# The first rows' normalization in a spectral and token-mixing kernel: Newton steps moved from GpSimd to VectorE, a longer first memset, and buffers exchanged in the later stages

## The chip, the core and the metric

The kernel runs on one core of one Trainium2 chip. The metric is device time in microseconds (us), from launch to the end of the program; the median of a few runs is compared. The core has TensorE (PE in the profile, with PEld for its weight loads), VectorE (DVE), ScalarE (ACT), GpSimd (POOL), and SyncE (SP), which issues most of the loads. ACT and POOL have DMA queues of their own beside SP's. Each engine runs its instructions in the order in which they were issued to it, and waits on semaphores for what the others produce.

## What is computed

```
xn = layernorm(x)                               x: 2048 x 640, fp32
a  = xn @ dft_hid_re.T ;  b = xn @ dft_hid_im.T             (640 x 640)
yA = dft_seq_re @ a - dft_seq_im @ b                        (2048 x 2048)
h  = layernorm(xn)
u  = gelu(h.T @ w1 + b1)                                    (640 x 1728)
yB = (u @ w2 + b2).T                                        (2048 x 640)
out = x + yA + yB
```

Two branches share the input: a Fourier mixing along both axes, and a mixer MLP along the token axis. Both begin with the layer norm of x.

## The kernel before

**Precision and splitting.** Every product is made from fp32 operands split in two: a high part rounded to the matmul's input type (`high`, an ACT copy, L151) and the low part, the rest (`low`, a VectorE subtraction, L154). Each product is three passes of matmuls: high with high, high with low, low with high (`three`, L162, L163, L165; `products` in the first columns, L511). Large products are done in the Strassen-Winograd manner, with 7 products of blocks in place of 8; the sums of blocks are VectorE's (`sub`, L157) and are spread between the steps.

**Steps.** The work is a list of steps. A step takes one tile of matrix rows ("piece", 128 x 512 or so), lets ACT make its top (high part) two steps ahead, VectorE its bottom (low part), and TensorE the matmuls. `turn_of` issues a turn in this order: loads, reads of finished banks, sums, the top of the step two ahead, extras, timed jobs, the bottom, what stands behind it, and then the step's matmuls. `JOBS_AT` and `LONG_AT` say in which turns a job from the waiting list is taken; loads, jobs and reads are hung on steps by number (`loads`, `timed`, `extras`, `behind_lo`).

**Stages.** First come the products of x with the sequence matrices (`first_columns` for the first block of 512 columns and the rows that arrive first, then `columns` for seven more blocks), stored to a scratch tensor y; then the hidden-axis products (`hidden`), then the up-projection (`up`, two stages) and the down-projection (`down`, two stages). Large buffers are eight "slabs" of on-chip memory, which take turns: rows of x with high and low parts (`fixed`), then the moving operands (`moving_of`), matrices (`load_matrices`) or extra pieces (`more`). A tile given a slab's tag waits for the last reader of the tile before it. Smaller pair buffers (`place`: v, ca, cb, x0, x1, x2) hold results that are summed up. Partial results of the up-projection go to a scratch tensor in HBM (`part_up`) from POOL's queue, and are summed there by the DMA.

**The start** is written out by hand in `START`, one word for one helper: `x` loads a row block of x (128 tokens x 640), `b` a piece of the matrices, `M` the two halves of the moments (L223), `A` their aggregate (L226), `R` the inverse root on ACT (L232), `O` the offset from it, `D` and `H` the high parts of a row's blocks, `N` the normalized row itself (ACT, L278), `L` the low parts (VectorE), `T` and `B` top and bottom of a step's piece, `P` the matmuls of a step, with a list of passes if not all three. The root from ACT's table is refined by a Newton step: three small operations and the offset. For rows 2, 3, 6 and 7 it is on VectorE (`F`: L238 to L240, L254). For rows 0, 1, 4 and 5 it is on POOL, in `factors_beside` (word `V`, L248 to L250 and L243), and the first offset too (`O`, L243). Row 0 is loaded in two halves (L536).

The first matrix piece, b0, is loaded from ACT's queue, behind a one-column memset of its tile (L498), so that the load waits for VectorE. Before the first real matmul, `WARM` matmuls on a zero tile run (L148): ten of 512 columns and four of 128.

The ten steps of `first_columns` are listed in `FIRST`. In the first step of both outputs the third pass stands last (`P0-0-1 P1-0-1 P0-2 P1-2`). Steps 0 to 5 are issued in `START`; from step 6 on the turns are made by `turn_of`. At the head of turn 6 ACT copies the first output's five banks (`read`, L519). Step 6 begins the second output's blocks 3 and 4 in banks 0 and 1, which the first output has used.

Of the kernel before, what the change touches and what calls it, by code (L numbers as in the profile page):

```python
# [8 lines left out]
F32 = mybir.dt.float32  # L9
# [15 lines left out]
G = 4  # L25
# [3 lines left out]
EPS = 1e-5  # L29
AHEAD = 2  # L30
LOADS = 4
WARM = 14

BLOCK = 10
APART = 2
# [12 lines left out]

START = """
    x0 b0 W0 b1 x1 b2 x4 b3 x5 b4 x2 x3 b5 x6 x7 b6 b7  # L50
    M0 A0 R0 T0 D0 O0 V0 H0 B0 T1 B1 M1 A1 N0 R1 T2 L0 O1 V1 H1 B2 P0-0-1 P1-0-1 P0-2 P1-2
    M4 A4 R4 N1 O4 V4 L1 T3 H4 B3 M5 A5 N4 R5 O5 V5 T4 P2
    L4 B4 P3 H5 T5 M2 A2 N5 M3 A3 R2-3 B5 F2-3 L5 q4 P4
    H2 T6 N2 M6 A6 B6 L2 q5 P5 T7 M7 B7 A7
"""


# [20 lines left out]
def fnet_plus_mixer(  # L78
# [38 lines left out]
    b2_sb = keep.tile([P, NS], F32, name="b2_sb")  # L117
    one = keep.tile([P, 1], F32, name="one")
    eps = keep.tile([P, 1], F32, name="eps")
    idea = keep.tile([P, 1], F32, name="idea")  # L120

    mv = keep.tile([P, NS, 2], F32, name="mv")
    norm = keep.tile([P, 2, NS], F32, name="norm")
# [16 lines left out]
    nc.vector.memset(idle, 0.0)  # L140
    nc.vector.memset(one, 1.0)
    nc.gpsimd.memset(eps, EPS)
    nc.gpsimd.tensor_scalar(idea, eps, EPS, eps, op0=ALU.add, op1=ALU.mult)
    psum = [acc.tile([P, CH], F32, name=f"psum{i}") for i in range(8)]
    for i in range(WARM):
        n = 4 if i < WARM - 4 else 1
        to = psum[7][:, : n * P].rearrange("p (n c) -> p n c", n=n)
        nc.tensor.matmul(to, idle, idle.unsqueeze(1).to_broadcast([P, n, P]), start=True, stop=True)  # L148

# [67 lines left out]

    stats = {}

    def statistics(k, row):  # L220
        stats[k] = small.tile([P, 2, 6], F32, name="st")
        for i in range(2):
            nc.vector.bn_stats(stats[k][:, i, :], row[:, i * H2 : (i + 1) * H2])  # L223

    def aggregate(k):
# [16 lines left out]
    def offset_beside(to, k):  # L242
        nc.gpsimd.tensor_scalar(to[:, 1, k : k + 1], mv[:, k, 0:1], to[:, 0, k : k + 1], -1.0, op0=ALU.mult, op1=ALU.mult)  # L243

    def factors_beside(k):

        r, q = small.tile([P, 1], F32, name="beside"), near[:, 0, k : k + 1]
        nc.gpsimd.tensor_scalar(r, mv[:, k, 1:2], EPS, q, op0=ALU.add, op1=ALU.mult)  # L248
        nc.gpsimd.tensor_scalar(r, r, q, -0.5, op0=ALU.mult, op1=ALU.mult)  # L249
        nc.gpsimd.tensor_scalar(norm[:, 0, k : k + 1], r, 1.5, q, op0=ALU.add, op1=ALU.mult)  # L250
        offset_beside(norm, k)

    def offset(to, ks):
        nc.vector.scalar_tensor_tensor(to[:, 1, ks], mv[:, ks, 0], -1.0, to[:, 0, ks], op0=ALU.mult, op1=ALU.mult)  # L254
# [103 lines left out]
    for q in range(4):  # L358
        place_fixed(0, q)

    def first_rows(k, which):
# [17 lines left out]
        for to, t in whole:  # L379
# [36 lines left out]
    def later_row(k):  # L416
        return later_pair(k % 4)[:, (k - 8) // 4, :]
# [69 lines left out]
    def first_columns():  # L487
# [6 lines left out]
        def load(i):  # L494
            m, k = FIRST[i][:2]
            to = raw[:, FIRST_AT[i], :]
            if i == 0:
                nc.vector.memset(to[:, :1], 0.0)  # L498
            (nc.sync if i else nc.scalar).dma_start(to, dft_seq[m * NC, k])

        def products(w, m, k, j0, j1, passes=(0, 1, 2)):
# [64 lines left out]
        def whole_row(k):  # L566
# [6 lines left out]

        return {
            "x": row, "b": load, "q": begin_loads, "T": top, "B": bottom, "P": run,
            "M": lambda k: statistics(k, x_in[k] if k < 8 else later_row(k)), "A": aggregate,
            "R": rooted, "F": factored, "O": lambda k: offset_beside(near, k), "V": factors_beside,
            "D": lambda k: first_hi(),
            "H": lambda k: first_rows(k, 0), "N": whole_row,
            "L": lambda k: first_rows(k, 1),  # L580
            "W": lambda k: nc.scalar.activation(one, one, AF.Abs_reciprocal_sqrt),
        }

    def columns(g, h, c):
# [13 lines left out]
        def load(name, q):  # L598
            i, m = int(name[1]) - 1, int(name[2]) - 1
            k = 8 * h + q + 4 * i  # L600
            if q >= 4:
                if not more_pairs:
                    more_pairs.append(keep.tile([P, 2, 2, 2, CH], F32, name="more", tag="slab1"))
                k = APART + q - 4 + 4 * i
            nc.sync.dma_start(b(name, q), dft_seq[m * NC + c, k])

# [161 lines left out]

    def load_matrices(qs):
        if 0 in qs:  # L770
            t = keep.tile([P, 3, 2, D], F32, name="hids", tag="slab0")
            raw_hid.update({q: t[:, q] for q in range(3)})
        for q in qs:
            if q > 2:
                raw_hid[q] = place["v"]()
            for m in range(2):
                nc.sync.dma_start(raw_hid[q][:, m, :], dft_hid[m, q])

    def matrices(q, tag):
# [262 lines left out]
    def up(stage, r, at):  # L1042
# [6 lines left out]
        def end(c):  # L1049
            if stage == 0:  # L1050
                nc.gpsimd.dma_start(part_up[r], c)
                for row, half, t in halves:
                    add_to(t, slice(TAIL if tail else P), row, half)
                return
            nc.gpsimd.dma_start(c, part_up[r], accum_op=ALU.add)

            def gelu(i):
                f = r + NF2 * i
                rows = P if f < NF else TAIL
                nc.scalar.activation(  # L1060
                    c[:rows, i, :], c[:rows, i, :], AF.Gelu_apprx_tanh, bias=b1_sb[:rows, f : f + 1]
                )
                if rows < P:

                    nc.gpsimd.memset(c[rows:, i, :], 0.0)


            e = s0 + 7
            late = 5 if tail else 2 if r >= 4 else 1
            for i in range(2):  # L1070
                timed[e + 6 + late + i].append(lambda i=i: gelu(i))
            if r < 4:
                timed[e + 9].append(lambda: jobs.extend(moving_of("down0", r, f"slab{4 + r}", lambda: c)))
            else:
                timed[e + 8 + late].append(lambda: nc.gpsimd.dma_start(part_up[r], c))

# [3 lines left out]
        def by_dram(i):  # L1080
            def run(row, half, b):

                at = i in (5, 7)
                t = place["x1"]()[:, (r + (i in (5, 4))) % 2, at * H2 : (at + 1) * H2]
                if not (tail and i in (5, 7, 4)):
                    nc.scalar.activation(t, b, AF.Copy)
                    if stage == 0:
                        halves.append((row, half, t))
                    else:
                        add_to(t, slice(P), row, half)  # L1090
                    return
# [75 lines left out]
    for q in range(3):  # L1167
        timed[s_half + 4 + 2 * q].append(lambda q=q: load_matrices((q,)))
    timed[s_half + 24].append(lambda: load_matrices((3,)))
    timed[s_half + 40].append(lambda: jobs.extend(  # L1170
        [j for q in range(4) for j in matrices(q, f"slab{(q + 1) % 4}")] + factors_again() + [lambda: load_matrices((4,))]
    ))
    timed[s_hid - 6].append(lambda: jobs.extend(matrices(4, "xb")))
    for t in range(NS):
# [2 lines left out]
        hidden(n, t, 0)  # L1177
    for q in range(4):
        get, changes, rest = rows_again(0, q, "v")
        timed[s_hid - 1].append(lambda js=[get, None, None] + changes + rest: jobs.extend(js))  # L1180
    loads[s_hid + 20].append(lambda: nc.sync.dma_start(b1_sb, b1))
    loads[s_hid + 21].append(lambda: nc.sync.dma_start(b2_sb, b2))
    s_up = len(steps)
# [8 lines left out]

    extras[len(steps) + 7].append(lambda: nc.scalar.activation(one, one, AF.Gelu_apprx_tanh))
    for r in range(NF2):
        up(1, r, ("x2", "ca", "cb", "v", "x0")[r % 5])
    s_down = len(steps)
    for t in range(NS // 2):
        down(0, t, ("cb", "x1")[t % 2])
    gets_hid, _, rests_hid = zip(*(hidden_rows(q, ("x0", "v")[q % 2]) for q in range(3)))
    for q in range(2):  # L1200
        timed[s_down + 7 + 2 * q].append(lambda q=q: jobs.append(gets_hid[q]))
    get_tail, rest_tail = tail_rows()
    timed[s_down + 14].append(lambda: jobs.extend(
        rests_hid[0] + [gets_hid[2], get_tail] + rests_hid[1] + rests_hid[2] + rest_tail
# [95 lines left out]
```

## Time and profile before

| | us |
|---|---|
| runs | 867.90, 867.87, 867.27; median 867.87 |
| profiled execution | 867.3 |
| its span, first to last instruction | 865.5 |
| TensorE busy | 860.3 |
| VectorE busy | 693.0 |
| ACT busy | 525.0 |
| POOL busy | 163.2 |

The span of the profiled execution is 1.8 us shorter than its time; the rest lies before the first instruction and behind the last. The granted clock of TensorE was 0.999 over the span. A timeline row gives the start, the duration, the engine, the line, the operation with its output and input, the count of merged instructions, and in brackets the idle time before it with what ended it. A row of the waits gives the waiting engine and line, the one that released it, the sum of the waits, their number and the longest.

### The profile page before, as it was taken

What the parts mean: (1) busy time and instruction counts of PE and PEld (TensorE: products, weight loads), DVE (VectorE), ACT (ScalarE), POOL (GpSimd) and SP (SyncE); (2) the same over time, 40 slices, a digit from 0 to 9 for tenths busy, and PEclk for the clock granted to TensorE, in tenths of its full rate; (3) what the DMA queues carried; (4) which work ended last, traced back from release to release, by engine and by line L of the source; (5) the groups of instructions that cost most, each with busy time, mean ns of one, the idle gap of its engine ahead of it and who ended that gap; (6) DMA issues with size and microseconds to landing.
All of it is one profiled execution on the core that took longest, in us unless ns stands there. A gap on an engine that the chain in (4) does not pass through costs nothing.

```text
span 865.5 us, 13915 instructions
## 1 busy us (share of the span) xinstructions
PE 860.3 (99%) x4898; PEld 789.2 (91%) x4898; DVE 693.0 (80%) x1173; ACT 525.0 (61%) x975; POOL 163.2 (19%) x224
## 2 busy tenths in 40 slices
PE   9999999999999999999999999999999999999998
PEld 6888888888888888889999999999999999999998
DVE  6798768757768888677877788888678978987887
ACT  6766576763455555547565556676667866555654
POOL 4222131210020211222110101111312221101211
PEclk9999999999999999999999999999999999999999
DMA  9949597695382746869586766665687689766776
GB/s 341 362 100 262 191 244 240 159 274 167 95 191 30 193 109 140 207 103 193 120 183 155 161 141 196 189 170 163 142 187 172 146 237 246 188 141 126 158 168 149
DMA packets 90293, 154.44 MB, mean 178 GB/s; under 512 B 9008, under 2 KB 37424, under 8 KB 89968
## 3 DMA queue, kind: packets, MB, share of 16 engines
q0 software_dynamic: 25008, 57.52, 36.5%
q1 hardware_dynamic: 64928, 95.70, 34.0%
q8 instruction: 38, 0.62, 0.3%
q10 hardware_dynamic: 288, 0.34, 0.1%
q14 instruction: 31, 0.25, 0.1%
HBM read 99.96 MB, written 58.82 MB: 183 GB/s over the span
## 4 chain that ended last, share of the span: by engine, by line
PE 98%; DMA 0%; POOL 0%; DVE 0%; ACT 0%; issue 0%; SPq 0%; DVEq 0%; ACTq 0%
PE psum L162 32%; PE psum L163 32%; PE psum L165 31%; PE psum L511 3%; DMA x<-in_x 0%; ACT x L278 0%; POOL beside L248 0%; POOL beside L249 0%; DVE n L154 0%; DVE st L223 0%; POOL near L243 0%; SPq L536 0%; DVE pair L951 0%; ACT near L232 0%; POOL norm L250 0%
## 5 line engine op out<-in xcount | busy, mean ns | idle before, releaser
L151 ACT ACTIVATE piece<-pieces 128x512 fp32r<-128x512 f32 (+2 forms) x472 | 295.5, 626 | 222.9 <-PE psum L165 137.5
L154 DVE TENSOR_TENSOR piece<-pieces,piece 128x512 fp32r<-128x512 f32 (+4 forms) x496 | 326.9, 659 | 128.2 <-ACT piece L151 125.0
L162 PE MATMUL psum<-piece,n 128*128 128x512 f32 x540 | 210.1, 389 | 0.0
L163 PE MATMUL psum<-piece,n 128*128 128x512 f32 x540 | 210.1, 389 | 0.0
L165 PE MATMUL psum<-piece,n 128*128 128x512 f32 x540 | 210.1, 389 | 0.0
L163 PE MATMUL psum<-sup,piece 128*128 128x320 f32 x392 | 120.8, 309 | 0.0
L162 PE MATMUL psum<-sup,piece 128*128 128x320 f32 x392 | 120.8, 309 | 0.0
L162 PE MATMUL psum<-sdown,piece 128*128 128x320 f32 x392 | 120.8, 309 | 0.0
L163 PE MATMUL psum<-sdown,piece 128*128 128x320 f32 x392 | 120.8, 309 | 0.0
L165 PEld LDWEIGHTS psum<-piece,n 128*128 128x128 f32 x540 | 101.3, 188 | 21.1
L162 PEld LDWEIGHTS psum<-piece,n 128*128 128x128 f32 x540 | 101.4, 188 | 21.1
L163 PEld LDWEIGHTS psum<-piece,n 128*128 128x128 f32 x540 | 101.4, 188 | 20.9
L157 DVE TENSOR_TENSOR pieces<-pieces 128x512 f32<-128x512 f32 (+3 forms) x142 | 111.9, 792 | 3.0
L165 PE MATMUL psum<-sup,piece 128*128 128x320 f32 x368 | 113.7, 309 | 0.0
L165 PE MATMUL psum<-sdown,piece 128*128 128x320 f32 x368 | 113.7, 309 | 0.0
L485 POOL DMA_DIRECT2D y<-c x65 | 56.0, 892 | 255.2 <-DVE c L688 153.9
L165 PE MATMUL psum<-shid,piece 128*128 128x320 f32 x280 | 86.5, 309 | 0.0
L163 PE MATMUL psum<-shid,piece 128*128 128x320 f32 x280 | 86.5, 309 | 0.0
L162 PE MATMUL psum<-shid,piece 128*128 128x320 f32 x280 | 86.5, 309 | 0.0
L162 PEld LDWEIGHTS psum<-sdown,piece 128*128 128x128 f32 x392 | 73.6, 188 | 0.0
L163 PEld LDWEIGHTS psum<-sup,piece 128*128 128x128 f32 x392 | 73.6, 188 | 0.0
L162 PEld LDWEIGHTS psum<-sup,piece 128*128 128x128 f32 x392 | 73.6, 188 | 0.0
(130 smaller groups left out, 1111.2 us busy)
## 6 DMA issues: line engine op xcount, KB each, us to landing
pieces<-in_dft_seq SPq DMA_DIRECT2D x119, 256.0 KB, 5.4
y<-c POOLq DMA_DIRECT2D x105, 256.0 KB, 4.9
pieces<-in_w SPq DMA_DIRECT2D x88, 256.0 KB, 4.2
out<-pair POOLq DMA_DIRECT2D x38, 320.0 KB, 5.9
pieces<-y SPq DMA_DIRECT2D x32, 320.0 KB, 4.7
pieces<-in_w SPq DMA_DIRECT2D x32, 192.0 KB, 2.7
out<-in_x SPq DMA_DIRECT2D x16, 320.0 KB, 8.1
up<-pair POOLq DMA_DIRECT2D x8, 640.0 KB, 3.2
```

The source lines that it names most:

```text
L151: nc.scalar.activation(hi, src, AF.Copy)
L154: nc.vector.tensor_sub(lo, src, hi.bitcast(F32))
L157: nc.vector.tensor_sub(to, a, b)
L162: nc.tensor.matmul(psum, wh, mh, start=first, stop=False, skip_group_check=True)
L163: nc.tensor.matmul(psum, wh, ml, start=False, stop=last and wl is None, skip_group_check=True)
L165: nc.tensor.matmul(psum, wl, mh, start=False, stop=last, skip_group_check=True)
L485: nc.gpsimd.dma_start(y_part[m][c][:, j, :], t, accum_op=ALU.add)
L511: nc.tensor.matmul(banks[m, j], channels(k, j)[rows], w[cols], start=n == 0 and k == begin, stop=n == 2 and k == end, skip_group_check=True,)
```

## The change

- The Newton steps of rows 0, 1, 4 and 5, with their offsets, go from POOL to VectorE: `V` is replaced by `F`, and the first offset (`O`) of rows 1, 4 and 5 goes to VectorE as well. Row 0's first offset stays on POOL (`G`).
- The order in `START` is rewritten. Row 1's moments (`M1-0`, `M1-1`) and row 0's low parts (`L0-0`, `L0-1`) are issued in halves that alternate; the moments of rows 2 and 3 stand later. The order of the matmuls in `START` is the old one.
- The memset ahead of b0 covers 384 columns in place of one. `WARM` is 12 in place of 14: two matmuls of 128 columns fewer.
- In the later stages, the slabs of `more` and of the hidden matrices are changed over, with the order of the slabs that `matrices` uses; x0 and x2 are exchanged in `up`'s second stage, x0 and v in `hidden_rows`, and `by_dram` uses x2 in the first up stage. The gelus of the first four blocks come one step later, the second hidden row's gather two steps later, and the gathers in `rows_again` one job later.

```diff
-WARM = 14
+WARM = 12
...
-    M0 A0 R0 T0 D0 O0 V0 H0 B0 T1 B1 M1 A1 N0 R1 T2 L0 O1 V1 H1 B2 P0-0-1 P1-0-1 P0-2 P1-2
-    M4 A4 R4 N1 O4 V4 L1 T3 H4 B3 M5 A5 N4 R5 O5 V5 T4 P2
-    L4 B4 P3 H5 T5 M2 A2 N5 M3 A3 R2-3 B5 F2-3 L5 q4 P4
-    H2 T6 N2 M6 A6 B6 L2 q5 P5 T7 M7 B7 A7
+    M0 A0 R0 T0 D0 G0 H0 B0 T1 F0 B1 N0 M1-0 T2 L0-0 M1-1 A1 R1 L0-1 O1 H1 F1 B2 N1 P0-0-1 P1-0-1 P0-2 P1-2
+    M4 L1 A4 T3 R4 O4 H4 B3 F4 T4 P2 N4 M5 B4 L4 T5 A5 R5 O5 H5 F5 P3
+    B5 M2 N5 L5 A2 T6 M3 B6 A3 R2-3 F2-3 q4 P4
+    H2 N2 M6 A6 L2 q5 P5 T7 M7 B7 A7
...
-    nc.gpsimd.tensor_scalar(idea, eps, EPS, eps, op0=ALU.add, op1=ALU.mult)
+    nc.gpsimd.tensor_scalar(near[:, 1, 0:1], eps, EPS, eps, op0=ALU.mult, op1=ALU.mult)
...
-        n = 4 if i < WARM - 4 else 1
+        n = 4 if i < WARM - 2 else 1
...
-    def factors_beside(k):
-
-        r, q = small.tile([P, 1], F32, name="beside"), near[:, 0, k : k + 1]
-        nc.gpsimd.tensor_scalar(r, mv[:, k, 1:2], EPS, q, op0=ALU.add, op1=ALU.mult)
-        nc.gpsimd.tensor_scalar(r, r, q, -0.5, op0=ALU.mult, op1=ALU.mult)
-        nc.gpsimd.tensor_scalar(norm[:, 0, k : k + 1], r, 1.5, q, op0=ALU.add, op1=ALU.mult)
-        offset_beside(norm, k)
...
-                nc.vector.memset(to[:, :1], 0.0)
+                nc.vector.memset(to[:, : 3 * P], 0.0)
...
-            "R": rooted, "F": factored, "O": lambda k: offset_beside(near, k), "V": factors_beside,
+            "R": rooted, "F": factored, "O": lambda k: offset(near, slice(k, k + 1)), "G": offset_beside,
...
-                    more_pairs.append(keep.tile([P, 2, 2, 2, CH], F32, name="more", tag="slab1"))
+                    more_pairs.append(keep.tile([P, 2, 2, 2, CH], F32, name="more", tag="slab0"))
...
-            t = keep.tile([P, 3, 2, D], F32, name="hids", tag="slab0")
+            t = keep.tile([P, 3, 2, D], F32, name="hids", tag="slab1")
...
-            late = 5 if tail else 2 if r >= 4 else 1
+            late = 5 if tail else 2
...
-                timed[e + 9].append(lambda: jobs.extend(moving_of("down0", r, f"slab{4 + r}", lambda: c)))
+                timed[e + 10].append(lambda: jobs.extend(moving_of("down0", r, f"slab{4 + r}", lambda: c)))
...
-                t = place["x1"]()[:, (r + (i in (5, 4))) % 2, at * H2 : (at + 1) * H2]
+                t = place["x1" if stage else "x2"]()[:, (r + (i in (5, 4))) % 2, at * H2 : (at + 1) * H2]
...
-        [j for q in range(4) for j in matrices(q, f"slab{(q + 1) % 4}")] + factors_again() + [lambda: load_matrices((4,))]
+        [j for q in range(4) for j in matrices(q, f"slab{(0, 2, 3, 1)[q]}")] + factors_again() + [lambda: load_matrices((4,))]
...
-        timed[s_hid - 1].append(lambda js=[get, None, None] + changes + rest: jobs.extend(js))
+        timed[s_hid - 1].append(lambda js=[None, get, None] + changes + rest: jobs.extend(js))
...
-        up(1, r, ("x2", "ca", "cb", "v", "x0")[r % 5])
+        up(1, r, ("x0", "ca", "cb", "v", "x2")[r % 5])
...
-    gets_hid, _, rests_hid = zip(*(hidden_rows(q, ("x0", "v")[q % 2]) for q in range(3)))
+    gets_hid, _, rests_hid = zip(*(hidden_rows(q, ("v", "x0")[q % 2]) for q in range(3)))
...
-        timed[s_down + 7 + 2 * q].append(lambda q=q: jobs.append(gets_hid[q]))
+        timed[s_down + 7 + 4 * q].append(lambda q=q: jobs.append(gets_hid[q]))
```

More of the change, by code (lines that the diff above doesn't have):

```diff
@@ L119, in fnet_plus_mixer @@
     eps = keep.tile([P, 1], F32, name="eps")
-    idea = keep.tile([P, 1], F32, name="idea")
     mv = keep.tile([P, NS, 2], F32, name="mv")
@@ L218, in fnet_plus_mixer, with statistics @@
     stats = {}
-    def statistics(k, row):
-        stats[k] = small.tile([P, 2, 6], F32, name="st")
-        for i in range(2):
+    def statistics(k, row, *halves):
+        if k not in stats:
+            stats[k] = small.tile([P, 2, 6], F32, name="st")
+        for i in halves or range(2):
             nc.vector.bn_stats(stats[k][:, i, :], row[:, i * H2 : (i + 1) * H2])
@@ L240, in inverse, with offset_beside @@
         nc.vector.scalar_tensor_tensor(to, r, 1.5, q, op0=ALU.add, op1=ALU.mult)
-    def offset_beside(to, k):
-        nc.gpsimd.tensor_scalar(to[:, 1, k : k + 1], mv[:, k, 0:1], to[:, 0, k : k + 1], -1.0, op0=ALU.mult, op1=ALU.mult)
-    def factors_beside(k):
-        r, q = small.tile([P, 1], F32, name="beside"), near[:, 0, k : k + 1]
-        nc.gpsimd.tensor_scalar(r, mv[:, k, 1:2], EPS, q, op0=ALU.add, op1=ALU.mult)
-        nc.gpsimd.tensor_scalar(r, r, q, -0.5, op0=ALU.mult, op1=ALU.mult)
-        nc.gpsimd.tensor_scalar(norm[:, 0, k : k + 1], r, 1.5, q, op0=ALU.add, op1=ALU.mult)
-        offset_beside(norm, k)
+    def offset_beside(k):
+        nc.gpsimd.tensor_scalar(
+            near[:, 1, k : k + 1], mv[:, k, 0:1], near[:, 0, k : k + 1], -1.0, op0=ALU.mult, op1=ALU.mult
+        )
     def offset(to, ks):
@@ L359, in fnet_plus_mixer, with first_rows @@
         place_fixed(0, q)
-    def first_rows(k, which):
+    def first_rows(k, which, *parts):
         a = fixed[0][k % 4]
@@ L378, in first_rows @@
             whole = whole[1:]
-        for to, t in whole:
+        for to, t in [whole[i] for i in parts] or whole:
             if which == 0 and k in LAST_ROWS:
@@ L575, in first_columns @@
             "x": row, "b": load, "q": begin_loads, "T": top, "B": bottom, "P": run,
-            "M": lambda k: statistics(k, x_in[k] if k < 8 else later_row(k)), "A": aggregate,
-            "R": rooted, "F": factored, "O": lambda k: offset_beside(near, k), "V": factors_beside,
+            "M": lambda k, *halves: statistics(k, x_in[k], *halves), "A": aggregate,
+            "R": rooted, "F": factored, "O": lambda k: offset(near, slice(k, k + 1)), "G": offset_beside,
             "D": lambda k: first_hi(),
             "H": lambda k: first_rows(k, 0), "N": whole_row,
-            "L": lambda k: first_rows(k, 1),
+            "L": lambda k, *parts: first_rows(k, 1, *parts),
             "W": lambda k: nc.scalar.activation(one, one, AF.Abs_reciprocal_sqrt),
```

## The prediction

> **What bounds the kernel now.** I read the page's totals first, then TensorE's own waits, then the timeline of the first 40 us. Totals and waits:
>
> ```profile
> span 865.5 us, 13915 instructions
> PE 860.3 (99%) x4898; PEld 789.2 (91%) x4898; DVE 693.0 (80%) x1173; ACT 525.0 (61%) x975; POOL 163.2 (19%) x224
> ...
> PE psum L148 <- DVE pieces L498: 1.0, 1, 1.0
> PE psum L511 <- ACT piece L151: 0.7, 1, 0.7
> PE psum L511 <- DVE n L154: 0.3, 1, 0.3
> ```
>
> TensorE is busy 99% of the span and waits three times in all, each time in the first 10.2 us. So the only time to be won lies before its first real matmul and in the wait at 10 us. Everything else in the diff can at best do nothing, or can add a wait where there is none. TensorE's timeline, start and duration:
>
> ```profile
> 1.00 4.23 PE L148 MATMUL psum<-idle 128*128 128x512 bf16 x14 [1.00 <-DVE pieces L498]
> 5.95 3.92 PE L511 MATMUL psum<-piece,n 128*128 128x512 f32 x16 [0.72 <-ACT piece L151]
> 10.14 23.87 PE L511 MATMUL psum<-piece,n 128*128 128x512 f32 x104 [0.27 <-DVE n L154]
> 33.85 0.39 PE L162 MATMUL psum<-piece,n 128*128 128x512 f32 x1
> 34.08 0.39 PE L163 MATMUL psum<-piece,n 128*128 128x512 f32 x1
> ```
>
> One 512-column matmul follows another every 0.227 us (33.85 to 34.08). The 16 of the first run (passes 0 and 1 of the first two steps) would take 16 x 0.227 = 3.63 us, so the next could go at 9.58 and goes at 10.14. From there 104 matmuls x 0.227 = 23.6 reach 33.75, and the row says 33.85: about 0.1 more is lost on the fifth of row 0. **To win at that wait: about 0.55 us at most.**
>
> **Part 1: the longer memset, and 12 warm matmuls for 14.** The first loads and the chain behind them:
>
> ```profile
> 0.75 0.87 SPq L536 DMA_DIRECT2D x<-in_x  x2
> 0.90 0.06 DVE L498 MEMSET pieces<- 128x1 f32 x1
> 1.01 0.38 ACTq L499 DMA_DIRECT2D pieces<-in_dft_seq  x1
> 3.14 0.49 DVE L223 BATCH_NORM_STATS2 st<-x 128x6 f32<-128x320 f32 x1 [2.17 <-DMA x<-in_x]
> 4.23 0.49 DVE L223 BATCH_NORM_STATS2 st<-x 128x6 f32<-128x320 f32 x1 [0.60 <-DMA x<-in_x]
> 5.07 0.29 ACT L232 ACTIVATE near<-mv,eps 128x1 f32<-128x1 f32 x1 [2.15 <-DVE mv L226]
> 5.27 0.61 ACT L151 ACTIVATE piece<-pieces 128x512 fp32r<-128x512 f32 x1
> ...
> 595.67 0.27 DVE L869 MEMSET pieces<- 128x256 f32 x1
> ...
> pieces<-in_dft_seq ACTq DMA_DIRECT2D x1, 256.0 KB, 2.7
> ```
>
> The first matrix tile (b0) is loaded from ACT's queue once the memset is done. It is issued at 1.01, between the two halves of row 0, which SP issues at 0.75 and about 1.19 (half of 0.87 later). The landings come in the order of the issues: first half before 3.14, b0 at 1.01 + 2.7 = 3.7, second half before 4.23. The memset of 384 elements costs, from 0.06 us for one and 0.27 for 256, about 0.38 (an estimate from these two rows), 0.32 more than now. So b0 is issued at 1.33, behind the second half. I take the two to change places: second half at about 3.6, b0 at about 4.2. VectorE then takes the second half's moments 0.6 us earlier; the bounds are 0 (the order of landing does not follow the issue) and 0.68 (the first half's moments occupy VectorE to 3.14 + 0.49 - 0.08 = 3.55). b0 is needed only at 5.27 - 0.6 = 4.67, behind its landing, and the whole chain of row 0 moves with the moments. **Gain 0.6 us.** The two warm matmuls left out end the warming some 0.1 us sooner, under TensorE's wait of 0.7: nothing.
>
> [...]
>
> **Part 2: Newton steps on VectorE.** Of POOL, 19 small operations go. Row 0's path to its low parts is now POOL to 8.41, ACT 8.44, VectorE 9.40. In the changed order VectorE does its lo of piece 0, Newton steps, the lo of piece 1, half of row 1's moments, then row 0's low parts. Durations:
>
> ```profile
> 6.05 0.68 DVE L154 TENSOR_TENSOR piece<-pieces,piece 128x512 fp32r<-128x512 f32 x1
> ...
> 9.40 0.89 DVE L154 TENSOR_TENSOR n<-x,n 128x512 fp32r<-128x512 f32 x2 [0.73 <-ACT x L278]
> 10.21 0.68 DVE L154 TENSOR_TENSOR piece<-pieces,piece 128x512 fp32r<-128x512 f32 x1
> 10.81 0.88 DVE L223 BATCH_NORM_STATS2 st<-x 128x6 f32<-128x320 f32 x2
> ...
> 19.41 0.21 DVE L226 BATCH_NORM_AGGREGATE mv<-st 128x2 f32<-128x12 f32 x1
> ...
> 20.10 0.15 DVE L238 SCALAR_TENSOR_TENSOR r<-mv,near 128x2 f32<-128x2 f32 x1
> ...
> 20.68 0.16 DVE L254 SCALAR_TENSOR_TENSOR norm<-mv,norm 128x2 f32<-128x2 f32 x1
> 20.75 0.89 DVE L154 TENSOR_TENSOR n<-x,n 128x512 fp32r<-128x512 f32 x2
> ```
>
> From start to start: a piece's lo 0.60 (10.21 to 10.81), a row's lo 0.81 (9.40 to 10.21; its parts 0.60 and 0.20), two moments 0.88 - 0.08 = 0.80, an aggregate 0.13, four Newton operations 0.65 (20.10 to 20.75), an offset 0.08. Row 0's first low part starts at 6.05 + 0.60 + 0.65 + 0.60 + 0.40 + 0.13 (waiting for ACT's normalized row) = 8.43 and ends near 9.1; TensorE wants it at 9.58. **The 0.55 at 10 us goes**, with row 1's parts in time too, by the same laying out.
>
> But VectorE now carries 4 x 0.65 + 3 x 0.08 = 2.8 us more before row 3's aggregate, the one at 19.41, which the new order also puts behind one more lo (B6). I laid its new order out with these steps, from 6.05 (before the 0.6 of part 1). Work up to the end of row 3's aggregate: to row 0's last low part 0.60 + 0.65 + 0.60 + 0.40 + 0.60 + 0.40 + 0.25 (aggregate behind its moments) + 0.20 = 3.70; then offset, Newton, lo of a piece, row 4's moments, row 1's lo, aggregate, 0.08 + 0.65 + 0.60 + 0.80 + 0.81 + 0.13 = 3.07; the same for row 4 with one more piece, 3.67; and for row 5, with the moments of rows 2 and 3 and one more piece, 0.08 + 0.65 + 0.60 + 0.80 + 0.81 + 0.13 + 0.80 + 0.60 + 0.21 = 4.68. In all 15.12. Waits: an offset now stands on VectorE right behind its own aggregate, and between them ACT must take the root; aggregate to root is 0.05 (19.62 to 19.67 below), the root 0.28, back 0.04, and VectorE could have begun 0.08 before its aggregate ended, so 0.45 to 0.47 each for rows 4 and 5, and 0.27 for row 1, where 0.20 of work lies between. Behind each the low parts queue, and wait for ACT's two roundings and normalization: 0.13, 0.26, 0.04 and 0.25. Together 1.89. Aggregate of row 3: 6.05 + 15.12 + 1.89 = **23.06, against 19.62 now: 3.44 us late.** What hangs on it, on ACT:
>
> ```profile
> 19.67 0.28 ACT L232 ACTIVATE near<-mv,eps 128x2 f32<-128x2 f32 x1
> 20.87 0.99 ACT L278 ACTIVATE n<-x,norm 128x256 fp32r<-128x256 f32 x2 [0.92 <-DVE norm L254]
> 21.77 0.61 ACT L151 ACTIVATE piece<-pieces 128x512 fp32r<-128x512 f32 x1
> 22.29 0.91 ACT L278 ACTIVATE x<-x,norm 128x640 f32<-128x640 f32 x1
> 23.10 0.61 ACT L151 ACTIVATE piece<-pieces 128x512 fp32r<-128x512 f32 x1
> 23.62 2.56 ACT L519 ACTIVATE c<-psum 128x512 f32<-128x512 f32 x5
> ```
>
> ACT takes rows 2 and 3's roots, row 2's roundings, row 2's normalization, the top of step 7, and only then the five copies that free the banks of the first output. The second half of step 6 begins in two of these banks. New: root at 23.11, Newton 23.43 to 24.17, roundings 24.20, then +0.90 +0.13 +0.81 +0.52: first copy at 26.56, done 0.59 later, 27.15. TensorE gets there after 24 + 15 + 9 + 15 + 15 + 9 = 87 matmuls, 5.95 + 0.1 + 87 x 0.227 = 25.8. **It waits about 1.4 us, then 0.25 for the second copy** (0.48 behind the first, less one matmul).
>
> A second wait follows at the first step of the next stage, whose second matmul (34.08) needs this lo:
>
> ```profile
> 32.35 0.69 DVE L154 TENSOR_TENSOR piece<-pieces,piece 128x512 fp32r<-128x512 f32 x1
> ```
>
> Between the copies at 23.62 and this lo, ACT and VectorE wait for each other in turn for 8.73 us, in an order that the change leaves. So it starts at 26.56 + 8.73 = 35.29 and ends at 35.98; the matmul of 34.08 goes at 36.04. **The path moves from the 0.55 gained to 1.96 late; with part 1, 1.96 - 0.6 = +1.36 us.** Behind that, VectorE and ACT are no further behind TensorE than now, so I add nothing.
>
> **Part 3: the late edits** (two slabs changed over, up-projection buffers exchanged, gelu and gathers later). TensorE waits nowhere after 10.14, so these can win nothing. Their cover:
>
> ```profile
> 699.82 0.31 PE L162 MATMUL psum<-sdown,piece 128*128 128x320 f32 x1
> 699.96 0.31 PE L163 MATMUL psum<-sdown,piece 128*128 128x320 f32 x1
> ...
> pairs<-up SPq DMA_DIRECT2D x2, 640.0 KB, 5.9
> ```
>
> A step of 12 such matmuls (0.14 to 0.15 each) is 1.8 us. The gathers move on SP's queue behind one load each, the gelus by one step on ACT; the second hidden row is read two steps (3.5 us) later and takes 5.9, but its first use is queued behind the first row's six jobs, at 3 of 7 steps, more than 10 steps on. Nothing, and up to 2 us if one comes a step late. The third passes already stand last in the old order: TensorE's order is the same but for the two warm matmuls.
>
> **Sum.** The profiled execution took 867.3 us, 865.5 of it span: 867.3 + 1.36 = 868.7. The three runs' median, 867.87, lies 0.57 above it; with about half of that I predict **868.9**. A measurement of this kernel can tell about 0.2% (1.7 us) from no change, so faster means under 866.1, slower over 869.6.
>
> **Rivals.**
> - *The lag never reaches TensorE* (0.12): the late aggregate is covered, and 0.6 + 0.55 are kept: 866.2. For it: VectorE idles in TensorE's first 20 us now; against: the sum above uses that idle time up.
> - *b0 does not change places* (0.18): 867.3 + 1.96 = 869.3, on the runs' level 869.5, half of it slower.
> - *Slower: the clock falls in the wait* (0.05). The first warm matmuls run slow: 10 of 512 and 4 of 128 columns take 4.23 us, where 0.227 each would be 2.5. If a wait of 1.4 to 1.7 us at 26 us brings that state back, it costs those 1.7 again: 870.4. [...]
> - *Slower: one late transfer arrives a step late* (0.07), at the end of the up-projection, where 640 KB take 5.9 us: +1.8, 870.5.
>
> **Chances and range.** Forecast 0.58; 0.11 of it lies above 869.6, since each of the seven waits is good to 0.1 only. Slower: 0.11 + 0.09 + 0.05 + 0.06 (nearly all of the last rival) = 0.31. Faster: the first rival with an earlier first half, 0.03. Same: 0.66. Low end: were none of VectorE's waits there (1.89 less on that chain), the lo at 35.98 would end at 34.1, the matmul go at 34.15, less 0.6: 866.8. High end: no gain from b0 and two more waits of 0.45 with the runs' 0.57: 867.3 + 1.96 + 0.9 + 0.2 = 870.4.
>
> **What would show it.** Right: first real matmul near 5.35; no wait near 10 us; TensorE waiting once on ACT L513 near 26 us and once on a DVE lo near 35 us; row 3's aggregate about 2.8 us later than 19.41; no wait after 40 us. Wrong: first matmul at 5.95 (b0 kept its place); no wait at 26 us (VectorE's order was cheaper than laid out); 512-column matmuls over 0.4 us apart after the wait (the clock); any TensorE wait after 500 us (a late transfer).

## The result, and the profile after

The changed kernel takes 870.39 us (median; 869.33 to 871.16), the kernel before, run beside it, 867.78: a ratio of 1.0028, 95% interval [1.0017, 1.004], so 0.28% slower. One execution of the changed kernel of 1434.86 us, at a granted clock of 0.556, is left out of the range and the ratio, as are single executions of over 2000 us in a later comparison. The profiled execution took 870.4 us, 868.6 of it span; before it was 867.3 and 865.5. The forecast was 868.9 (866.8 to 870.4).

In the changed kernel a line number stands for an earlier one of the kernel before: matmul L505 (L511) in the first stage, L161, L162 and L164 (L162, L163, L165) in the columns, the rounding L150 (L151), the lo L153 (L154), the copies out of the banks L513 (L519). The totals, and below them TensorE's waits (us in total, times, longest):

```profile
span 868.6 us, 13911 instructions
PE 862.5 (99%) x4896; PEld 790.5 (91%) x4896; DVE 695.6 (80%) x1192; ACT 526.3 (61%) x975; POOL 154.9 (18%) x205
```

```profile
PE psum L147 <- DVE idle L139: 1.0, 1, 1.0
PE psum L505 <- ACT piece L150: 0.8, 1, 0.8
PE psum L162 <- DVE piece L153: 0.3, 1, 0.3
```

The wait for row 0's low parts has gone, as meant. In its place stands one for a low part (lo) that VectorE makes in the next stage. TensorE's timeline shows where, and that the first real matmul is later, not earlier (6.48 against 5.95):

```profile
1.00 4.66 PE L147 MATMUL psum<-idle 128*128 128x512 bf16 x12 [1.00 <-DVE idle L139]
6.48 29.19 PE L505 MATMUL psum<-piece,n 128*128 128x512 f32 x120 [0.82 <-ACT piece L150]
35.51 0.39 PE L161 MATMUL psum<-piece,n 128*128 128x512 f32 x1
36.24 0.50 PE L162 MATMUL psum<-piece,n 128*128 128x512 f32 x1 [0.34 <-DVE piece L153]
```

The second matmul of the first column step, 34.08 before, goes at 36.24: 2.16 late. The matmuls next to it add 0.15, and nothing is lost from there to the last matmul, 2.31 late. The timelines of VectorE and ScalarE give the chain behind it (start, duration, and in brackets the idle time ahead and what ended it):

```profile
3.13 0.89 DVE L223 BATCH_NORM_STATS2 st<-x 128x6 f32<-128x320 f32 x2 [1.76 <-DMA x<-in_x]
...
6.46 0.69 DVE L153 TENSOR_TENSOR piece<-pieces,piece 128x512 fp32r<-128x512 f32 x1 [1.04 <-ACT piece L150]
...
23.10 0.20 DVE L226 BATCH_NORM_AGGREGATE mv<-st 128x2 f32<-128x12 f32 x1
...
35.50 0.68 DVE L153 TENSOR_TENSOR piece<-pieces,piece 128x512 fp32r<-128x512 f32 x1
```

```profile
4.36 0.29 ACT L232 ACTIVATE near<-mv,eps 128x1 f32<-128x1 f32 x1 [1.05 <-DVE mv L226]
5.80 0.63 ACT L150 ACTIVATE piece<-pieces 128x512 fp32r<-128x512 f32 x1 [1.15 <-DMA pieces<-in_dft_seq]
...
23.34 0.30 ACT L232 ACTIVATE near<-mv,eps 128x2 f32<-128x2 f32 x1 [2.02 <-DVE mv L226]
...
26.82 2.52 ACT L513 ACTIVATE c<-psum 128x512 f32<-128x512 f32 x5
```

Row 0's moments now run back to back from 3.13, and its root is taken at 4.36 instead of 5.07. But ScalarE then has nothing to round: the first matrix tile lands only at 5.78. The transfers' view gives its time from issue to landing, 2.7 before:

```profile
pieces<-in_dft_seq ACTq DMA_DIRECT2D x1, 256.0 KB, 4.4
```

From VectorE's first lo (6.46) its new load of work leads to row 3's aggregate at 23.10 (19.41 before), to the copies at 26.82 (23.62) and to the lo at 35.50 (32.35), for which TensorE waits.

The rest of the loss, 0.8, lies behind the last matmul. The last matmul and the issue of the last store, before and after:

```profile
862.03 0.31 PE L163 MATMUL psum<-sdown,piece 128*128 128x320 f32 x1
...
862.96 0.35 ACTq L1121 DMA_DIRECT2D out<-pair  x1
```

```profile
864.35 0.31 PE L162 MATMUL psum<-sdown,piece 128*128 128x320 f32 x1
...
865.28 0.35 ACTq L1115 DMA_DIRECT2D out<-pair  x1
```

Both issues stand 0.93 behind their matmul, but the span ends 868.6 - 865.3 = 3.3 us behind the one and 865.5 - 863.0 = 2.5 behind the other. So 2.31 + 0.81 = 3.12 make up the 3.1 between the two profiled executions. The transfers' view of that last store, before and after, shows where about half of the 0.81 lies:

```profile
out<-pair ACTq DMA_DIRECT2D x1, 80.0 KB, 1.6
```

```profile
out<-pair ACTq DMA_DIRECT2D x1, 80.0 KB, 2.0
```

It takes 2.03 us from issue to landing instead of 1.64, which is 0.39. The other 0.42 lies between its landing and the end of the span (1.32 against 0.90).

### The profile page after: what moved, and what is told of

Its sections match the earlier page's. It is cut to its first block, busy times and chain, and to the rows that moved or that the text cites. A ratio compares the mean times of both kernels' runs of the same rounds, so it can differ in the third digit from the quotient of the medians.

```text
span 868.6 us, 13911 instructions
## 1 busy us (share of the span) xinstructions
PE 862.5 (99%) x4896; PEld 790.5 (91%) x4896; DVE 695.6 (80%) x1192; ACT 526.3 (61%) x975; POOL 154.9 (18%) x205
## 4 chain that ended last, share of the span: by engine, by line
PE 95%; DMA 2%; DVE 1%; ACT 1%; SPq 0%; issue 0%
PE psum L162 32%; PE psum L161 32%; PE psum L164 31%; DMA x<-in_x 1%; DMA pieces<-in_dft_seq 1%; DMA later<-in_x 1%; DVE piece L153 0%; ACT c L513 0%; ACT n L272 0%; DVE st L223 0%; SPq L493 0%; DVE n L153 0%; ACT piece L150 0%; ACT x L272 0%; SPq L532 0%
## 5 line engine op out<-in xcount | busy, mean ns | idle before, releaser
L153 DVE TENSOR_TENSOR piece<-pieces,piece 128x512 fp32r<-128x512 f32 (+4 forms) x496 | 326.9, 659 | 130.1 <-ACT piece L150 126.9
L150 ACT ACTIVATE piece<-pieces 128x512 fp32r<-128x512 f32 (+2 forms) x472 | 295.4, 626 | 220.4 <-PE psum L164 138.5
L162 PE MATMUL psum<-piece,n 128*128 128x512 f32 x540 | 210.2, 389 | 0.3 <-DVE piece L153 0.3
L161 PE MATMUL psum<-piece,n 128*128 128x512 f32 x540 | 210.1, 389 | 0.0
L164 PE MATMUL psum<-piece,n 128*128 128x512 f32 x540 | 210.1, 389 | 0.0
L162 PEld LDWEIGHTS psum<-piece,n 128*128 128x128 f32 x540 | 101.3, 188 | 21.8 <-DVE piece L153 0.8
L162 PE MATMUL psum<-sup,piece 128*128 128x320 f32 x392 | 120.8, 309 | 0.0
L161 PE MATMUL psum<-sup,piece 128*128 128x320 f32 x392 | 120.8, 309 | 0.0
L162 PE MATMUL psum<-sdown,piece 128*128 128x320 f32 x392 | 120.8, 309 | 0.0
L161 PE MATMUL psum<-sdown,piece 128*128 128x320 f32 x392 | 120.8, 309 | 0.0
L161 PEld LDWEIGHTS psum<-piece,n 128*128 128x128 f32 x540 | 101.4, 188 | 21.2
L164 PEld LDWEIGHTS psum<-piece,n 128*128 128x128 f32 x540 | 101.4, 188 | 20.9
L164 PE MATMUL psum<-sup,piece 128*128 128x320 f32 x368 | 113.7, 309 | 0.0
L164 PE MATMUL psum<-sdown,piece 128*128 128x320 f32 x368 | 113.7, 309 | 0.0
L164 PE MATMUL psum<-shid,piece 128*128 128x320 f32 x280 | 86.5, 309 | 0.0
L162 PE MATMUL psum<-shid,piece 128*128 128x320 f32 x280 | 86.5, 309 | 0.0
L161 PE MATMUL psum<-shid,piece 128*128 128x320 f32 x280 | 86.5, 309 | 0.0
L161 PEld LDWEIGHTS psum<-sup,piece 128*128 128x128 f32 x392 | 73.6, 188 | 0.0
L161 PEld LDWEIGHTS psum<-sdown,piece 128*128 128x128 f32 x392 | 73.6, 188 | 0.0
L162 PEld LDWEIGHTS psum<-sup,piece 128*128 128x128 f32 x392 | 73.6, 188 | 0.0
```

The costliest lines, as they stand in the source:

```text
L150: nc.scalar.activation(hi, src, AF.Copy)
L153: nc.vector.tensor_sub(lo, src, hi.bitcast(F32))
L161: nc.tensor.matmul(psum, wh, mh, start=first, stop=False, skip_group_check=True)
L162: nc.tensor.matmul(psum, wh, ml, start=False, stop=last and wl is None, skip_group_check=True)
L164: nc.tensor.matmul(psum, wl, mh, start=False, stop=last, skip_group_check=True)
```

## The experiments

The theory under test (V): three more rows' Newton steps in VectorE's order make row 3's moments, then the bank copies, then the first column step late, and this sets the end wherever the first matmul stands. Its rivals: the late first tile (M) or the slow first matmuls are the loss (the expectations call these two together theory S); or the late edits are.

**1. The short memset back in the changed kernel.**

```
-                nc.vector.memset(to[:, : 3 * P], 0.0)
+                nc.vector.memset(to[:, :1], 0.0)
```

> The changed kernel with the memset ahead of b0 back at one column; all else as changed. Theory V (VectorE's longer order in the start sets when the first stage ends): b0 lands near 3.7 us again and the first real matmul goes at 5.95, at full rate; no wait near 10 us; TensorE then waits for the bank copies near 26 us (1.4 us, then 0.25) and for a lo near 35 us (about 0.8); the second matmul of the first column step goes at 36.0, as late as in the changed kernel (36.2), and the time stays 2 us over the kernel before, 869.5 to 870. Theory S (the loss is b0's late landing and the slow clock behind it): no wait at 26 us, that matmul at 33.6, and a time 0.5 us under the kernel before, 867.3.

Measured: 870.19 us, ratio to before 1.0028 [1.0018, 1.0038]. TensorE's timeline and one row of VectorE's:

```profile
5.89 19.98 PE L505 MATMUL psum<-piece,n 128*128 128x512 f32 x87 [1.13 <-ACT piece L150]
26.96 8.05 PE L505 MATMUL psum<-piece,n 128*128 128x512 f32 x33 [1.10 <-ACT c L513]
...
35.75 0.50 PE L162 MATMUL psum<-piece,n 128*128 128x512 f32 x1 [0.51 <-DVE piece L153]
```

```profile
22.62 0.20 DVE L226 BATCH_NORM_AGGREGATE mv<-st 128x2 f32<-128x12 f32 x1
```

The first real matmul is 0.6 earlier than in the change, and the time is the same. After 87 matmuls TensorE waits for the copies, as forecast: 1.26 and then 0.37 beyond the usual steps of 0.227 (1.4 and 0.25 forecast), and 0.78 more at the lo. Where TensorE starts early it waits near 26 us, where it starts late it comes to the banks when they are free. V holds, and M falls as the main cause: with the first tile in time, the second matmul of the first column step goes at 35.75, still 1.67 later than before and only 0.49 earlier than in the change. The medians (870.19 and 870.39) do not tell that 0.49 from nothing. The 87 matmuls in 19.98 us run at the full rate (0.228 apart), so slow first matmuls are not the loss either.

**2. The late edits alone, on the kernel before** (slabs, buffers, gelus, gathers as in the diff's last ten places).

> The kernel before with the late edits alone (slabs changed over, buffers exchanged, gelus and gathers later). Both theories: no TensorE wait after 10.2 us, before as now, and the kernel before's time within 0.4 us: 867.4 to 868.2. If a late transfer is the cause: a TensorE wait after 500 us, or a longer tail behind the last matmul, and up to 870.

Measured: 867.70 us, ratio 0.9999 [0.9991, 1.0008]. Nothing that can be told from noise, as forecast; the interval reaches some 0.7 us to each side. In its profiled execution TensorE waits nowhere after 10.2 us. The stretch behind the last matmul is 0.4 longer than before, which run 10, with the same edits, does not repeat.

**3. The start edits alone** (the change with the late edits undone).

> The changed kernel with the late edits taken back, so the start's edits alone. Both theories: the changed kernel's time, 870 to 870.6, with the second matmul of the first column step at 36.0 to 36.4 and no TensorE wait behind it. If the late edits had a part: 0.5 us or more below the changed kernel.

Measured: 869.68 us, ratio 1.0024 [1.0015, 1.0033]. In the profiled execution the first tile took 2.9, and here the prediction's own case can be seen whole:

```profile
5.29 20.00 PE L505 MATMUL psum<-piece,n 128*128 128x512 f32 x87 [0.16 <-ACT piece L150]
26.38 8.04 PE L505 MATMUL psum<-piece,n 128*128 128x512 f32 x33 [1.08 <-ACT c L513]
...
35.16 0.50 PE L162 MATMUL psum<-piece,n 128*128 128x512 f32 x1 [0.52 <-DVE piece L153]
```

First matmul at 5.29 (forecast 5.35), the wait at the copies, the matmul behind the lo at 35.16 (forecast 36.04 - 0.6 = 35.44). Two waits, at 452.7 (0.25) and 650.6 (0.79 beyond the usual step), that neither before nor after has, cost some 1 us in this execution. They can't be put down to the missing late edits: experiments 5, 6 and 7, which have these edits, lose 0.6 to 0.7 in a wait at 404 to 409 us that neither before nor after has. The median is 0.71 below the changed kernel's, more than the 0.5 that was to speak for a part of the late edits; but the kernel before was 0.44 lower in this comparison too (867.34 against 867.78) and the intervals overlap, so such a part is not shown.

**4. The memset and the 12 warm matmuls alone, on the kernel before.**

```
-WARM = 14
+WARM = 12
...
-        n = 4 if i < WARM - 4 else 1
+        n = 4 if i < WARM - 2 else 1
...
-                nc.vector.memset(to[:, :1], 0.0)
+                nc.vector.memset(to[:, : 3 * P], 0.0)
```

> The kernel before with the memset of 384 columns and 12 warm matmuls alone; Newton steps on POOL and the old order. Row 0's second half lands near 3.5 us and b0 near 5.8. Theory V: the first real matmul at 6.5, 0.5 later than before; the 0.55 us wait near 10 us is gone, since row 0's low parts come 0.3 to 0.7 us earlier; VectorE's chain has 1 us to spare at the first column step, so that step's second matmul goes at 34.1 and the time is the kernel before's, 867.5 to 868.3, plus 1.7 in those executions in which the first 8 matmuls run at the slow rate. Theory S: the changed kernel's whole loss, 870 to 870.5, in the median.

Measured: 867.64 us (866.33 to 869.46), ratio 1.0001 [0.9992, 1.001]. The profiled execution had its first tile late again, and its first matmul at 6.91:

```profile
pieces<-in_dft_seq ACTq DMA_DIRECT2D x1, 256.0 KB, 4.8
```

```profile
6.91 27.49 PE L511 MATMUL psum<-piece,n 128*128 128x512 f32 x120 [1.25 <-ACT piece L151]
```

The gap at 10 us was gone without any edit to VectorE's order, because TensorE started 0.96 later; the first column step came only 0.40 later than before. Its eleven executions spread evenly over 3.1 us, where 22 of the 30 of before lie between 867.0 and 867.6. This fits an uncertain landing of the first tile: with the long memset it took 2.9 to 4.8 us in four profiled executions, with the short one and the old order of loads 2.6 to 2.8 in before and in experiments 1, 2, 7 and 8.

**5. Row 0 alone on VectorE**: the change with the short memset, rows 1, 4 and 5 back on POOL in the old order.

```
-    M0 A0 R0 T0 D0 G0 H0 B0 T1 F0 B1 N0 M1-0 T2 L0-0 M1-1 A1 R1 L0-1 O1 H1 F1 B2 N1 P0-0-1 ...
-    M4 L1 A4 T3 R4 O4 H4 B3 F4 T4 P2 N4 M5 B4 L4 T5 A5 R5 O5 H5 F5 P3
-    B5 M2 N5 L5 A2 T6 M3 B6 A3 R2-3 F2-3 q4 P4
+    M0 A0 R0 T0 D0 G0 H0 B0 T1 F0 B1 N0 M1-0 T2 L0-0 M1-1 A1 R1 L0-1 G1 V1 H1 B2 P0-0-1 ...
+    M4 A4 R4 N1 G4 V4 L1 T3 H4 B3 M5 A5 N4 R5 G5 V5 T4 P2
+    L4 B4 P3 H5 T5 M2 A2 N5 M3 A3 R2-3 B5 F2-3 L5 q4 P4
```

> The changed kernel with the short memset, and the Newton steps and first offsets of rows 1, 4 and 5 back on POOL, in the old order of the start; row 0's stay on VectorE, with row 1's moments and row 0's low parts in halves. Theory V (the loss is VectorE's longer order from row 1 on): first real matmul at 5.9, no wait near 10 us, no wait at 26 or 35 us, second matmul of the first column step at 33.5 (34.08 before), time 0.5 us under the kernel before: 866.6 to 867.0. Rival (the split halves of row 1, or the late edits, carry the loss): waits of TensorE remain near 26 and 35 us, and 869 or more.

Measured: 867.45 us, ratio 1.0001 [0.9992, 1.001]. No wait near 10, 26 or 35 us but 0.15 at 11.5, and row 3's aggregate at 19.10 (before 19.41, experiment 1 22.62):

```profile
5.99 27.69 PE L513 MATMUL psum<-piece,n 128*128 128x512 f32 x120 [0.32 <-ACT piece L150]
33.52 0.39 PE L161 MATMUL psum<-piece,n 128*128 128x512 f32 x1
```

```profile
19.10 0.21 DVE L226 BATCH_NORM_AGGREGATE mv<-st 128x2 f32<-128x12 f32 x1
```

Against experiment 1 this puts the 3.5 us on the three later rows and their order. It also shows that row 0's Newton step on VectorE, with row 1's moments and row 0's low parts in halves, closes the gap at 10 us at no cost that can be told. But it takes back two things at once. From its first lo to row 3's aggregate VectorE takes 16.64 us in experiment 1 and 13.01 here; of what stands ahead of that aggregate only there, the three rows' Newton steps and offsets are 2.2 us by the steps of the prediction, and the lows of two pieces (`B5`, `B6`) and of row 5 (`L5`), which the new order puts there, are 2.0. The Newton steps on VectorE in the old order were not tried, so the shares of the two stay open. Of the 0.33 that the first column step came earlier (33.52 against 33.85) the end had nothing: it lost 0.58 once, at 405 us, in a wait for a ScalarE tile, and 0.4 behind the last matmul. The median is 0.45 above the top of what was expected.

**6. The same with the long memset.**

> The same with the memset of 384 columns. b0's landing varies: where it lands near 4.3, the first real matmul goes at 5.25 and the time is 866.0 to 866.4; where it lands near 6, it goes at 6.5 to 6.9 and the time is 867.2 to 867.8, or 1.7 more where the clock is still slow. If b0's late landing is a chance of single executions: runs spread over 2 us or more, against 0.6 for the kernel with the short memset.

Measured: 867.73 us (866.94 to 869.49), ratio 1.0002 [0.9993, 1.0011]. Here the profiled execution had the first tile in time, and the gain of part 1 shows:

```profile
pieces<-in_dft_seq ACTq DMA_DIRECT2D x1, 256.0 KB, 2.9
```

```profile
5.41 27.67 PE L513 MATMUL psum<-piece,n 128*128 128x512 f32 x120 [0.50 <-ACT piece L150]
32.91 0.39 PE L161 MATMUL psum<-piece,n 128*128 128x512 f32 x1
```

The first column step is 0.94 earlier than before, yet the median is that of before. This execution, 867.41, is no faster either, against the 866.0 to 866.4 expected: 0.65 is lost again in the wait at 405 us, and 0.42 behind the last matmul.

**7. The first offsets of rows 1, 4 and 5 back on POOL** (O1, O4, O5 become G1, G4, G5; short memset).

> The changed kernel with the short memset and only the first offsets of rows 1, 4 and 5 back on POOL; the Newton steps stay on VectorE. It tells VectorE's waits (three, 0.27 + 0.47 + 0.47) from its work (four Newton steps, 2.6). If the work is the cost: the waits near 26 and 35 us stay as they are or grow a little, since POOL's offset (0.26 to 0.7) takes the place of the wait on the way to the high parts: 869.8 to 870.6. If the waits are the cost: 1.2 us less, 868.6 to 869.2.

Measured: 870.11 us, ratio 1.0032 [1.002, 1.0045]. Nothing is won: VectorE waits for the same root one instruction later, at the Newton step, as row 5's shows:

```profile
18.22 0.16 DVE L238 SCALAR_TENSOR_TENSOR r<-mv,near 128x1 f32<-128x1 f32 x1 [0.36 <-ACT near L232]
```

Row 3's aggregate comes at 23.05. So the place of the offsets is not the cost; since the wait for the root moved and did not go, how the 3.5 us divide into work and waits for the root isn't told apart by this. The profiled execution, 871.38 where the others took 870.05 to 870.14, shows something more. TensorE's timeline, and a table of windows (stretch, its length, busy time and count of PE, PEld, DVE, ACT and POOL, then TensorE's granted clock, DMA share and GB/s):

```profile
27.39 9.66 PE L505 MATMUL psum<-piece,n 128*128 128x512 f32 x33 [1.57 <-ACT c L513]
```

```profile
27.40:28.70 1.30, 1.30 (x4) 0.85 (x5) 1.30 (x4) 1.30 (x4) 1.04 (x2) 0.96 0.00 0
28.70:31.30 2.60, 2.60 (x8) 1.98 (x7) 1.97 (x8) 2.09 (x7) 1.99 (x4) 0.50 0.84 288
31.30:34.00 2.70, 2.70 (x12) 2.21 (x11) 2.00 (x5) 1.25 (x3) 0.00 (x0) 0.87 1.01 325
```

After the wait 33 matmuls take 9.66 us instead of the 8.05 of experiment 1. From 28.7 to 31.3 the granted clock is 0.50. That is the rival "the clock falls in the wait", with its price (1.6; 1.7 was forecast), in one execution.

**8. The copies before rows 2 and 3** in the changed kernel (short memset): their roots, Newton steps, roundings, normalization and lows move behind the five copies.

> The changed kernel with the short memset, and the root, Newton steps, roundings, normalization and low parts of rows 2 and 3 moved behind the five bank copies. Theory V, place of the first wait (the copies stand on ACT behind row 2's work): the wait at 26 us goes; but the moved work now stands ahead of the next pieces' tops and lows, so TensorE waits 1.5 us or more between 30 and 34 us and again at the first column step, whose second matmul goes at 36 to 37: 870 to 870.8. If the wait at 26 us stays, the place is wrong.

Measured: 871.02 us, ratio 1.0046 [1.0033, 1.0058].

```profile
33.85 1.94 PE L505 MATMUL psum<-piece,n 128*128 128x512 f32 x6 [1.22 <-ACT piece L150]
...
37.02 0.50 PE L162 MATMUL psum<-piece,n 128*128 128x512 f32 x1 [1.00 <-DVE piece L153]
```

No wait at 26 us any more, so that wait is the one for the copies; but the same work is then late at 32.2 and 35.6, and more is lost (871.02, where up to 870.8 was expected). This order of the copies is no way out.

**9 and 10. A version meant to beat both**: row 0 alone on VectorE, and its second half on ScalarE's queue ahead of the first tile, in place of the long memset. Run 9 has the late part of before, run 10 that of the change.

```
-                    nc.sync.dma_start(x_in[0][:, i * H2 : (i + 1) * H2], x_rows[0][:, i * H2 : (i + 1) * H2])
+                    (nc.scalar if i else nc.sync).dma_start(x_in[0][:, i * H2 : (i + 1) * H2], x_rows[0][:, i * H2 : (i + 1) * H2])
```

> The kernel before (its late part unchanged) with row 0's Newton step on VectorE, row 1's moments and lo parts halved, 12 warm matmuls, and the second half of row 0 loaded by ACT's queue ahead of the first matrix tile, so that it lands early without the long memset. Rows 1, 4 and 5 keep their Newton steps on POOL, in the order of before. If the cost of the change is the three later rows' Newton work on VectorE and only that: second half landed by 3.6, first real matmul near 5.35 (5.95 before), at most 0.15 lost near 10 us, no wait at 26 or 35 us, first matmul of the first column step near 32.9 (33.85 before), the end 0.9 to 1.0 earlier: 866.4 to 866.8. If the first matrix tile, now issued last, lands behind 4.7: first real matmul later by as much, 867.3 or more. If an earlier start always brings a wait at 26 us (TensorE reaches the banks before the copies have freed them, as the copies depend on rows 2 and 3 only): a wait there of up to 0.9 and no gain, 867.4.

> The same start as the run beside it, with the late edits of the change as well. The late edits cost nothing by the theory: the same time as beside it, 866.4 to 866.8, with no wait of TensorE near 400 to 650 us. If the end behind the last matmul grows by 0.4 with the late edits, as in the run of the late edits alone (3.9 against 3.5): 866.8 to 867.2.

Measured: 867.28 us, ratio 0.9998 [0.9989, 1.0007], and 867.01, ratio 0.9994 [0.9985, 1.0004]. The expectation's second case came true: the tile, issued last, took 4.0 and 4.7, and ScalarE waits for it. Run 9's rows of ScalarE and TensorE:

```profile
5.24 0.63 ACT L151 ACTIVATE piece<-pieces 128x512 fp32r<-128x512 f32 x1 [0.16 <-DMA pieces<-in_dft_seq]
```

```profile
5.92 27.61 PE L512 MATMUL psum<-piece,n 128*128 128x512 f32 x120 [0.38 <-ACT piece L151]
33.37 0.39 PE L162 MATMUL psum<-piece,n 128*128 128x512 f32 x1
```

TensorE runs through the first stage without a gap from its first real matmul on in both. In run 9 that leaves 0.48 at the first column step, which is below what can be measured; in run 10 the first matmul goes at 6.64, and the first column step is 0.24 later than before. No version here is shown to be faster than the kernel before.

## Why the prediction was right or wrong

**The wait at 10 us**: right. It went, and experiment 5 shows that row 0's Newton step on VectorE, with the halves, is enough for that.

**Part 1, a gain of 0.6 with b0 landing at about 4.2**: right for the half row, wrong for b0. The second half landed at 3.46 and the root came 0.71 earlier, but b0 took 4.4 us, not 2.9, so VectorE's chain began at 6.46 instead of the 5.45 forecast. This is the term that was mis-sized: +1.0 (in experiment 3, with b0 in time, the matmul behind the lo goes at 35.16, in the change at 36.24). I took b0's 2.7 us from an execution in which it was issued ahead of the second half and moved it on by its issue; with b0 behind that half, six profiled executions gave 2.9, 2.9, 4.0, 4.4, 4.7 and 4.8 (with b0 ahead 2.6 to 2.8). The rival "b0 keeps its place" fell too. Why b0 behind the half row took 4.0 to 4.8 us in four executions and 2.9 in two is not shown by any run here.

**Part 2, VectorE 3.4 us late, seen at the copies and at the lo**: right in mechanism, place and size. In experiments 1 and 3, where TensorE starts in time, both waits stand where the prediction put them, and the matmul behind the lo goes at 35.75 and 35.16 against 36.04 and 35.44 laid out: the chain was reckoned 0.3 too long. Row 3's aggregate is 2.6 later than before in experiment 3 (22.03), where about 2.8 was named. One reading in the words is short: the new order puts not only `B6` ahead of that aggregate but `B5` and row 5's low parts too; the sum of 15.12 has all three. So the size is that of the whole new order, and not of the Newton steps alone. In the changed kernel's own profile the wait at 26 us is missing, which the prediction named as a sign of a cheaper order. It is missing because TensorE was late itself: first matmul at 6.48, and its first eight at half rate (0.427 apart from the second on, 0.227 behind them). Behind this the same chain holds TensorE at the lo, so the late start hardly shows in the end.

**Part 3, the late edits at nothing**: right as far as can be measured (experiment 2). Whether they matter in the changed order is not shown (experiment 3).

**Not foreseen**: the 0.81 behind the last matmul. It was 3.5 in before and in experiments 4, 9 and 10, 3.9 in 2, 5, 6 and 7, 4.1 to 4.5 in 1, 3, 8 and the change, a single execution each. It comes in two parts. The last store takes 1.6 us from issue to landing in before and in experiments 4, 6, 7, 9 and 10, and 1.9 to 2.6 in 1, 3, 8 and the change. In the change a load of instructions (queue q14 in the transfers' view, one packet between 865.2 and 865.7) begins while that store is under way; in before none does. From the landing to the end it is 0.9 in before and in 3, 4, 9 and 10, and 1.3 in the change and in 1, 6, 7 and 8. The late edits alone do not set it (run 10 has them, and 3.5). That the instruction load slows the store is not shown, and why the change has both parts stays open; the tail was left out of the sum because its instructions are the same.

**The sum**: +1.36 was forecast for the profiled execution and +3.12 came: 1.36 + 0.8 at the lo (1.0 from b0, less 0.2 of the chain) + 0.15 in the matmuls next to it + 0.81 behind the last matmul. Between the medians it is 2.6. That 870.39 lies in the range, by 0.01, is luck: the top of 870.4 was made of no gain from b0, two more waits on VectorE and 0.2 for the runs' level (where the words name 0.57), and what came was b0 a further 0.4 late and the 0.81. **The rivals**: the clock's fall did not happen in the change, but once in experiment 7; the late transfer and the covered lag did not come. The likeliest case, within 0.2% (up to 869.6), was missed by 0.8 on the side that had 0.31.

## What to carry to other kernels

Here work was taken off a side engine and put into the order of an engine that is 80% busy. For the one urgent item that cost nothing that can be told: row 0's step closed the gap. The other three rows, for which TensorE had not waited while they were on POOL, and the order written for them put a new wait 16 us later. Read which items are late, and try those alone first. And where two loads are issued 0.2 us apart at the start, as b0 and row 0's half are here, a delay of one exchanged a landing after 2.6 to 2.8 us for one after 2.9 to 4.8; the worth of that is a range, not the difference of two landings in one execution.

## What the runs showed of the hardware that was not expected

The granted clock of 0.50 in experiment 7 came 28.7 us in, after TensorE had waited 1.74 and 0.37 within 2.5 us. It is one execution: in experiments 1, 3 and 8, with waits of 1.2 to 1.4, the granted clock was 1.00 from 24 to 32 us (1 and 3) and from 26 to 40 (8). What made it fall in the one and not in the others is not shown.

The first real matmuls of the changed kernel ran at half rate without the granted clock showing it. In experiment 7 the column shows it (0.50 from 28.7 to 31.3), and the 33 matmuls there take 1.6 us longer than in experiment 1. In the profiled execution of the changed kernel the first real ones start 0.427 apart from 7.08 to 10.06, 0.227 from there, and the table of windows has a clock of 1.00 for both:

```profile
7.00:10.00 3.00, 3.00 (x8) 2.31 (x7) 2.84 (x10) 1.78 (x3) 0.00 (x0) 1.00 1.03 392
10.00:12.00 2.00, 2.00 (x10) 1.58 (x9) 1.69 (x9) 1.52 (x4) 0.00 (x0) 1.00 1.04 408
```

Eight matmuls in 3 us, then ten in 2: the distance of the starts tells the rate there, the clock column does not. It is one execution: in experiment 4, after the same twelve warm matmuls and a longer pause (1.25 us idle against 0.82), the real ones run at the full rate (0.228 apart).
